# Chunked attention in front of a gated MLP: exponentials one head at a time on ScalarE, with the maximum as bias and the sum as by-product, heads paired by half, and all steps in a new order

## The chip, the core and the metric

One core of a Trainium2 chip runs the whole program. The metric is the device time of one execution in microseconds (us). Engines: PE is TensorE (PEld its weight loads), DVE is VectorE, ACT is ScalarE, POOL is GpSimd, SP is the engine that here only issues DMAs.

## The reference

A chunked attention with 8 heads, then a gated MLP that mixes along the sequence. Batch 4, 768 tokens, head size 64, chunks of 32 queries that see 8 memory keys and 56 keys around the chunk (16 to the left, 8 to the right).

```python
for c in range(nc):                                   # 24 chunks of 32 queries
    scores = scale * np.matmul(q_c, k_full.transpose(0, 1, 3, 2))
    scores = scores - np.max(scores, axis=-1, keepdims=True)
    a = np.exp(scores)
    a = a / (np.sum(a, axis=-1, keepdims=True) + 1e-09)
    out[:, :, c_start:c_end] = np.matmul(a, v_full)
...
h = gelu_tanh(x @ w_in)                               # x: (4, 768, 512), w_in: (512, 1024)
u, v = (h[..., :d_ff // 2], h[..., d_ff // 2:])
v_n = (v - mu) / np.sqrt(var + 1e-06) * g_ln
v_s = np.einsum('ts,bsd->btd', w_sg, v_n) + b_sg[None, :, None]
return (x + (u * v_s) @ w_out)
```

## The kernel before

The program is written as named steps, and the string `ORDER` says in which order they are recorded. Each engine then runs its own steps strictly in that order, so `ORDER` is a program for five queues at once. A star behind a name gives the step to the second engine it may run on.

**Attention** goes in 24 units `u` (4 batches, 6 tiles of 128 queries; unit `u` belongs to batch `u // 6`). A unit loads `q`, `k`, `v` (SP), and then runs
- `S`: 32 score matmuls into the PSUM tile `sav`, for 8 heads of 64 keys;
- `mx` the row maxima (DVE), `sb` the scores less the maximum, from `sav` to the SBUF tile `e` (DVE), `ex` one exponential over the 128x512 tile (ACT), `z` zeros for keys that do not exist at the ends of a sequence (POOL), `sm` the sums (DVE), `sa`/`sr` epsilon and reciprocal (DVE), `nm` the normalisation (DVE or POOL);
- `T` and `p`: four 128x128 transposes on PE and a copy (ACT or DVE) for the first ten units; `yt` and DMAs `E` for the others;
- `A`: 32 matmuls with `v`, again into `sav`;
- `xc` a copy to `x` (ACT), `xh` the high part (ACT), `xl` the low part (DVE or POOL). For four units (`DIRECT`) `xh` and `xl` read `sav` themselves.

There is one tile `sav` of two PSUM banks. Each bank holds the scores of four heads in its first half and the results of `A` in its second. Every step that touches `sav`, on PE, DVE or ACT, waits until the step of another engine that touched it last is through.

**The MLP** runs every product three times, on high and low parts (`HL`). Per batch: `V` six products of 12 matmuls with 512 columns, `U` eight of 12 with 384, `W` eight of 18, `O` eight of 12; behind each V and U come two ACT and two or more DVE steps (`v1` to `v9`, `u1` to `u4`), behind W `w1` to `w4`, behind O `o1` and the store. Names carry batch, half or tile, and block: `W001` is batch 0, half 0, block 1. Five PSUM tiles `mm` hold the products.

**Weights** arrive as float64 and are decoded by steps `d1` to `d9` on DVE, ACT and POOL: four blocks each of the two halves of `w_in` (`i1x`, `i0x`) and four of `w_out` (`ox`). The half `i1x` is needed by the first V. `ga`/`gb` split `w_sg`. `zz5` records five idle matmuls on `ident` that keep PE warm where there is nothing to do.

Of the kernel before, what the change touches and what calls it, by code (L numbers as in the profile page):

```python
# [39 lines left out]
d6i01 xh0 zz6 k5 d7i13 mx3 q5 xl0 sb3 nm2* A1 d8i13 ex3 S4 v4 xc1 d9i13* T2 xh1 k6 d2i03 V00 d1i03 q6 d4i03  # L40
xl1* p2 d2i02 d3i03 d6i03 d4i02 cbh sm3 mx4 V01 v100 sa3 sb4 sr3 v200 ex4 sm4 v300 v400 nm3* S5 v101 sa4
v500 A2 d7i01 v201 q7 T3 k7 mx5 v301 zz6 v5 sr4 xc2 d7i00 vx00 v401 p3 vy00 sb5 xh2 v600 v501 d8i00 S6 nm4*
ex5 xl2 d8i01 vx01 k8 mx6 A3 z5 q8 vy01 d9i01 sm5 T4 v6 xc3 V02 sa5 sr5 xh3 p4* d9i00 sb6 d6i02 v601 ex6
d5i03 z6 A4 v701 nm5* sm6 v801 S7 v7 xc4 sa6 sr6 xh4 mx7 q9 nm6* T5 k9 xl4 zz2 p5 sb7 xl3 V04 ex7 d1i02
d7i03 sm7 d3i02 sa7 sr7 d5i02 T6 d8i03 S8 v901* p6 v700 A5 v104 d7i02* k10 V03 v800 q10 nm7* v204 xh5 v8 mx8
v304 xl5 d9i03 xc5 d8i02 sb8 v404 ex8 v900 T7 v504 A6 sm8 d9i02 v102 S9 vx04 v9 xc6 p7* V05 v202 k11 ga50
q11 ga21 mx9 v302 vy04 sa8 sb9 v604 ga10 ga01 sr8 v402 nm8* ga31 U010 ga20 v502 ga41 v704 ex9 gb01 vx02 v804
vy02 sm9 U001 gb31* v602 g11 sa9 gb20* g00 v702 g30 sr9 v904* v802 U002 nm9 v105 gb10* ga11 v205 v902 g51
ga00 A7 v305 gb21* ga30 S10 gb11 v405 v103 g40 T8 v10 xc7 v203 gb00 k12 u1010 U003 v505 v303 q12 u2010 gb30
ga51 vx05 u1001 v403 u3010 gb51 vy05 u2001 u1002 U013 u4010 ga40 v605 v503 u3001 u1003 v705 u4001 v805 U000  # L50
vx03 u2003 vy03 v905* u3003 v603 mx10 v703 U012 u4003 v803 sb10 v903 u2002 ex10 p8* u3002 U011 sm10 u4002
sa10 d1o0 sr10 gb40* d3o0 T9 gb50* u1012 A8 d5o0 u1011 p9 W001 nm10* u2012 ro1 xc8 u2011 v11 u3012 u3011
gb41* d7o0 u4012 u1013 u4011 u2013 d8o0 W012 w1001 u3013 d2o1 u4013 d4o1 d1o1 w2001 d3o1 d6o1 w3001 d5o1
W002 w1012 w4001 ro2 w2012 d7o1 u1000 w3012 u2000 u3000 d9o0* d8o1 W000 u4000 w4012 w1002 d9o1 w2002 w3002
d1o2 d2o2 d3o2 w4002 W003 d4o2 w1000 d5o2 d6o2 w2000 ro3 d7o2* w3000 w4000* d8o2 W010 w1003 d9o2* w2003
w3003 d1o3 w4003* S11 d3o3 d2o3 w1010 W013 d4o3 q13 mx11 k13 w2010 d6o3 w3010 d5o3 sb11 w4010 A9 yt10 ex11
d7o3* S12 z11 v12 w1013 d8o3 W011 sm11 q14 d9o3* k14 sa11 w2013 sr11 mx12 w3013 nm11* sb12 O003 w1011 w4013
ex12 yt11 z12 w2011 Ec5 sm12 w3011 O000 o1003 w4011 sa12 sr12 nm12 out003 O011 Ed5 o1000 S13 o1011 Ea5 O013
mx13 sb13 ex13 S14 k15 o1013 Eb5 sm13 O012 mx14 sa13 sr13 nm13 O002 q16 o1012 k16 out012 out013 q15 O001
o1002 out000 yt12 out011 out002 yt13 sb14 O010 xh7 o1001 xh6 xl7* out001 ex14 xl6 xh8 sm14 V11 o1010 xl8*  # L60
out010 sa14 sr14 nm14* xc9 xh9 U102 v111 xl9* v211 v311 U101 u1102 v411 u2102 v511 u3102 u4102 V12 u1101
vx11 vy11 u2101 v611 u3101 v711 u4101 v811 v911* U100 v112 v212 v312 V13 v412 u1100 u2100 v512 u3100 u4100
vx12 vy12 v612 A10 v113 v712 V10 v213 v812 v13 xc10 v912 v313 xh10 v413 xl10 v513 A11 v110 vx13 vy13 S15
v210 v613 Ec6 xc11 V14 v713 v310 mx15 xh11 v410 v813 xl11* q17 v913* k17 v510 V15 v114 Ed6 sb15 vx10 v214
# [5 lines left out]
w1110 A13 w2110 k20 mx18 W111 w3110 q20 xc13 w4110* Ed7 Ea7 W102 w1111 w2111 w3111 w4111 v16 Ec7 O110 w1102  # L70
w2102 w3102 w4102 O112 o1110 Eb7 W100 o1112 out110 out112 yt16 W103 w1100 yt17 w2100 sb18 w3100 w4100* ex18
A14 w1103 z18 sm18 S19 v17 xc14 w2103 O111 sa18 k21 mx19 w3103 q21 sr18 w4103 sb19 ex19 nm18 O101 o1111 sm19
out111 sa19 sr19 nm19* O100 o1101 out101 O102 o1100 out100 A15 o1102 S20 out102 Eb8 O103 mx20 O113 q22 o1103
xh14 Ea8 xh12 xl14* xh13 xl12 V22 o1113 xl13* out113 v18 Ed8 V20 v122 v222 v322 Ec8 v422 U200 v522 v120 vx22
v220 out103 vy22 v320 v622 k22 U203 v420 u1200 u2200 v520 u3200 yt18 V21 u1203 u4200 xc15 sb20 xh15 yt19
ex20 xl15 u2203 vx20 sm20 u3203 A16 u4203 sa20 vy20 V23 v722 v620 v19 xc16 sr20 nm20* v822 xh16 v922* xl16*
v121 A17 v720 v221 V24 v820 Ea9 xc17 v920* v321 v123 v421 xh17 v223 xl17 v521 v323 U202 Ed9 vx21 v423 vy21
v523 v621 V25 v721 u1202 vx23 Ec9 v821 vy23 u2202 v623 u3202 v921 u4202 v723 v124 U211 Eb9 v823 v224 v923*
v324 v125 v424 U212 u1211 v225 v20 u2211 v325 v524 u3211 v425 U213 u1212 u4211 v525 yt20 A18 vx25 u2212
u1213 vx24 vy25 u3212 u2213 S21 v625 vy24 v21 xc18 u4212 v624 U201 u3213 mx21 q23 k23 u4213 v725 sb21 v825  # L80
A19 v724 u1201 ex21 v925 S22 u2201 v22 xc19 sm21 U210 v824 mx22 u3201 v924* u4201 sa21 W212 sb22 sr21 ex22
nm21 sm22 yt21 sa22 Ec10 sr22 nm22* W210 w1212 w2212 w3212 w4212 Ed10 u1210 W201 w1210 u2210 u3210 Ea10
u4210 w2210 w3210 W202 w1201 w4210* Eb10 w2201 w3201 w4201* W203 w1202 w2202 w3202 w4202* yt22 A20 w1203
W213 w2203 v23 xc20 w3203 w4203* A21 w1213 W200 w2213 w3213 w4213 W211 w1200 w2200 w3200 w4200 O201 w1211
# [531 lines left out]
```

## Time and profile before

| | |
|---|---|
| time, median of 3 runs | 407.88 us (403.1 to 409.68) |
| time of the profiled execution | 405.58 us |
| its span, first to last instruction | 403.8 us |
| mean granted TensorE clock | 0.992 |
| busy: PE, DVE, ACT, POOL | 379.8, 285.8, 160.8, 104.4 us |

The span is 1.8 us shorter than the time of that same execution. A row of the timeline reads: start, duration, engine, operation, tile written <- tiles read, and in brackets the idle time before it with what ended it. Durations of instructions that follow each other overlap by a little, so the distance from start to start is the better price of one. Each float32 matmul of the attention shows as two records (x64 for 32 matmuls).

### The profile page before, as it was taken

The numbers are of one execution on the slowest core, as the hardware profiler recorded it, in microseconds if no ns is written. First come the engines' busy times: TensorE is split into PE (matmuls) and PEld (weight loads), VectorE is DVE, ScalarE is ACT, GpSimd is POOL, SyncE is SP. The second block draws the span as 40 slices with busy tenths as digits, with TensorE's granted clock in tenths as the row PEclk, the third lists the DMA queues.
The fourth block names the chain that finished last, engine by engine and source line by source line (L and its number), as shares of the span: only waits on it lengthen the run. The fifth ranks groups of instructions, "written<-read, shape, count | busy, mean of one in ns | idle before, by whom it ended". The sixth has DMA issues, their size and how long they took to land.

```text
span 403.8 us, 11335 instructions
## 1 busy us (share of the span) xinstructions
PE 379.8 (94%) x4896; PEld 353.5 (88%) x4896; DVE 285.8 (71%) x558; ACT 160.8 (40%) x296; POOL 104.4 (26%) x113
## 2 busy tenths in 40 slices
PE   7788788999989999999999999998999999999996
PEld 6776677989979998789999988988999988999995
DVE  4996889999989567897637358895636456756532
ACT  4554646676532045653312046652211156532100
POOL 1433565463603021331121113321011224130000
PEclk9996999999999999999999999999999999999999
DMA  7998463542134360443143343242111320000022
GB/s 282 398 396 279 128 212 131 176 157 102 56 117 128 101 226 2 141 145 119 39 125 120 131 136 118 53 170 63 44 54 41 100 71 2 1 2 0 2 78 79
DMA packets 24530, 47.66 MB, mean 118 GB/s; under 512 B 4384, under 2 KB 13600, under 8 KB 24480
## 3 DMA queue, kind: packets, MB, share of 16 engines
q1 hardware_dynamic: 24480, 46.94, 35.0%
q8 instruction: 38, 0.62, 0.6%
q14 instruction: 12, 0.10, 0.1%
HBM read 36.96 MB, written 6.29 MB: 107 GB/s over the span
## 4 chain that ended last, share of the span: by engine, by line
PE 69%; DVE 19%; DMA 4%; issue 3%; ACT 3%; POOL 1%; SPq 0%; DVEq 0%; POOLq 0%; ACTq 0%
PE mmc L109 13%; PE mma L109 13%; PE mmd L109 12%; PE mmb L109 11%; PE mme L109 11%; PE sav L109 8%; DVE ga L109 2%; DMA y<-in_w_out 2%; DVE gb L109 2%; DMA rawc<-in_w_in 2%; DVE xo L109 1%; DVE rdb L109 1%; DVE w_sg_lo L109 1%; DVE eb L109 1%; ACT ga L109 1%
## 5 line engine op out<-in xcount | busy, mean ns | idle before, releaser
L109 PE MATMUL mma<-ident 128*128 128x128 f32 x136 | 18.3, 295 | 1.4 <-POOL mhalf L109 1.4
L109 PEld LDWEIGHTS mma<-ident 128*128 128x128 f32 x136 | 17.2, 208 | 1.7 <-POOL mhalf L109 1.4
L109 PEld LDWEIGHTS sav<-pt,va 64*64 64x64 f32 x512 | 8.5, 135 | 8.4 <-DVE ea L109 2.6
L109 PE MATMUL sav<-pt,va 64*64 64x32 f32 x512 | 9.4, 221 | 6.4 <-DVE eb L109 2.0
L109 PE MATMUL sav<-ka,qa 64*32 64x64 f32 x768 | 10.8, 231 | 4.3 <-DMA qa<-in_qs 1.5
L109 PEld LDWEIGHTS sav<-ka,qa 64*32 64x32 f32 x768 | 8.7, 109 | 6.2 <-issue 4.2
L109 PEld LDWEIGHTS sav<-pt,vb 64*64 64x64 f32 x512 | 9.1, 143 | 5.5 <-ACT w_in_hi L109 1.8
L109 ACT ACTIVATE eb<-eb 128x512 f32<-128x512 f32 x12 | 7.6, 630 | 16.0 <-DVE eb L109 15.9
L109 PE MATMUL sav<-pt,vb 64*64 64x32 f32 x512 | 10.1, 228 | 3.1 <-ACT w_in_hi L109 1.6
L109 ACT ACTIVATE gb<-gb 128x512 f32<-128x512 f32 (+1 forms) x14 | 8.8, 632 | 8.2 <-DVE gb L109 8.1
L109 PE MATMUL sav<-kb,qb 64*32 64x64 f32 x768 | 10.3, 224 | 1.9 <-DVE exb L109 1.9
L109 PEld LDWEIGHTS sav<-kb,qb 64*32 64x32 f32 x768 | 8.4, 105 | 3.4 <-DVE exb L109 2.0
L109 ACT ACTIVATE ga<-ga 128x512 f32<-128x512 f32 (+1 forms) x14 | 8.9, 633 | 6.0 <-DVE ga L109 5.9
L109 DVE SCALAR_TENSOR_TENSOR mmc<-mmc,g_half,b_half 128x384 f32<-128x384 f32 x8 | 5.0, 622 | 8.3 <-PE mmc L109 8.3
L109 POOL TENSOR_TENSOR rsc<-rsc,mhalf 128x1 f32<-128x1 f32 x8 | 4.4, 550 | 24.6 <-DVE rsc L109 24.6
L109 ACT COPY xa<-sav 128x512 f32<-128x512 f32 x9 | 5.2, 583 | 13.6 <-PE sav L109 10.9
L109 PE MATMUL mma<-w_in_hi,paira 128*128 128x512 f32 x32 | 9.9, 435 | 0.0
L109 PEld LDWEIGHTS sav<-pt,vc 64*64 64x64 f32 x512 | 8.3, 135 | 1.8 <-issue 1.2
L109 ACT ACTIVATE ea<-ea 128x512 f32<-128x512 f32 x12 | 7.6, 631 | 5.7 <-DVE ea L109 5.5
L109 POOL TENSOR_TENSOR rsb<-rsb,mhalf 128x1 f32<-128x1 f32 x8 | 4.4, 548 | 18.7 <-DVE rsb L109 15.9
L109 PE MATMUL sav<-pt,vc 64*64 64x32 f32 x512 | 9.2, 221 | 0.0
L109 POOL TENSOR_TENSOR rsa<-rsa,mhalf 128x1 f32<-128x1 f32 x8 | 5.0, 627 | 16.0 <-DVE rsa L109 16.0
(604 smaller groups left out, 1268.2 us busy)
## 6 DMA issues: line engine op xcount, KB each, us to landing
...
pt<-y SPq DMA_DIRECT2D x112, 32.0 KB, 1.9
...
```

Of the source, the lines that this page charges most:

```text
L109: return self.tc.keep_in_program_order(getattr(self.engine, name)(*args, **kw))
```

## The change

The exponential takes the scores from PSUM itself, one head at a time, eight instructions per unit on ACT: the negated maximum, times 0.125, is the bias of each, and each sums its row as a by-product. So `sb` and `sm` go; `mb` (a multiplication of 128x8 maxima) comes; missing keys get -1e30 in `sav`, on DVE ahead of the maximum, instead of zeros in `e` on POOL. Scores and results are paired by half of the heads instead of by neighbours, so that the copies out of `sav` keep its order. And `ORDER` is a new one throughout.

```diff
 ORDER = """
-ri10 k0 ri12 zz18 q0 ro0 v2 ri11 k1 g01 d1i10 d2i10 g31 d3i10 d4i10 d5i10 q1 d6i10 d1i12 ri00 d7i10* d3i12
-S0 d2i12 ri13 d8i10 zz19 d5i12 d4i12 d2o0 d9i10 mx0 k2 d4o0 sb0 d6o0 g21 ex0 d6i12 z0 d2i11 q2 d1i11 d4i11
+ri11 v0 q0 zz13 k0 k1 ri13 q1 v1 g40 d2i11 d1i11 d4i11 d3i11 d6i11 d5i11 d7i11* S0 d8i11 zz13 d9i11 k2 z0
+mx0 g31 q2 mb0 d2i13 ex0 d1i13 d4i13 S1 sa0 sr0 d3i13 d6i13 zz7 q3 mx1 nm0* ri12 mb1 ri03 ex1 d5i13 k3 T0
...
                         eng.matmul(
-                            s_v[CH * c:CH * c + CH, r, m], q[64 * r:64 * r + 64, m, c],
+                            s_v[CH * c:CH * c + CH, r, 2 * (m % 2) + m // 2], q[64 * r:64 * r + 64, m, c],
...
+        def no_keys(eng):
+            if tt == 0:
+                eng.memset(s_v[0:CH, :, :, 0:16], -1e30)
+            else:
+                eng.memset(s_v[P - CH:P, :, :, 56:64], -1e30)
+
         def largest(eng):
             eng.tensor_reduce(
-                mx.rearrange("p (r m) -> p r m", r=2), s_v, axis=AX.X, op=ALU.max
+                mx.rearrange("p (r m) -> p r m", r=2), s_v, axis=AX.X, op=ALU.max, negate=True
             )
-        def less(eng):
-            eng.tensor_tensor(
-                e_v, s_v, mx.rearrange("p (r m) -> p r m", r=2).unsqueeze(3).broadcast_to([P, 2, 4, KW]),
-                op=ALU.subtract,
-            )
...
+        def exps(eng):
+            for r in range(2):
+                for m in range(4):
+                    g = slice(4 * r + m, 4 * r + m + 1)
+                    eng.activation(
+                        e[:, 4 * r + m], s_v[:, r, m], AF.Exp, scale=0.125, bias=mx[:, g], accum_out=rd[:, g]
+                    )
...
+        if tt in (0, NTT - 1):
+            step(f"z{u}", no_keys, vector)
         step(f"mx{u}", largest, vector)
-        step(f"sb{u}", less, vector)
-        step(f"ex{u}", lambda eng: eng.activation(e, e, AF.Exp, scale=0.125), scalar)
-        if tt in (0, NTT - 1):
-            step(f"z{u}", no_keys, gpsimd)
-        step(f"sm{u}", lambda eng: eng.tensor_reduce(rd, e, axis=AX.X, op=ALU.add), vector)
+        step(f"mb{u}", lambda eng: eng.tensor_scalar_mul(mx, mx, 0.125), vector)
+        step(f"ex{u}", exps, scalar)
...
-        def by_pair(x):
-            return x[:, :, sl].rearrange("p (a h) t -> p a h t", h=2)
+        def by_half(x):
+            return x[:, :, sl].rearrange("p (h a) t -> p h a t", h=2)
...
-        step(f"xc{u}", lambda eng: eng.copy(by_pair(x32), av_x), scalar)
+        step(f"xc{u}", lambda eng: eng.copy(by_half(x32), av_v), scalar)
```

Three places of the new order follow, as rows of one engine's program. First DVE in the opening, before: the maximum `mxa` and the subtraction that writes `ea` of unit 0, and its sums `rda`, stand among the steps that decode blocks of `w_in` (`mc`, `exb`, ...) and `w_out` (`xo`).

```order
L109 TENSOR_REDUCE mxa<-sav 128x8
L109 TENSOR_TENSOR ea<-sav,mxa 128x512
L109 SCALAR_TENSOR_TENSOR xo<-y,xo 128x512
L109 SCALAR_TENSOR_TENSOR exc<-rawc,exc 128x512
L109 TENSOR_SCALAR exb<-rawb 128x512
L109 TENSOR_SCALAR mb<-rawb 128x512
L109 TENSOR_TENSOR mc<-mc,exc 128x512
L109 SCALAR_TENSOR_TENSOR exb<-rawb,exb 128x512
L109 SCALAR_TENSOR_TENSOR mb<-rawb,mb 128x512
L109 TENSOR_TENSOR w_in_lo<-mc,w_in_hi 128x512
L109 TENSOR_REDUCE rda<-ea 128x8
```

The same place of DVE's program in the changed kernel (here `mxa` scaled is the step `mb0`; the tiles `md`, `exd` belong to block i13):

```order
L108 MEMSET sav 32x2x4x16
L108 TENSOR_REDUCE mxa<-sav 128x8
L108 TENSOR_SCALAR mxa<-mxa 128x8
L108 TENSOR_SCALAR exd<-rawd 128x512
L108 TENSOR_SCALAR md<-rawd 128x512
L108 TENSOR_SCALAR rda<-rda 128x8
L108 RECIPROCAL rda<-rda 128x8
L108 SCALAR_TENSOR_TENSOR exd<-rawd,exd 128x512
```

Two rows of 128x512 per unit have gone, and the memset on `sav` has come.

Next ACT at the same place. Before, after the first decode steps, one exponential of unit 0 over all of `ea`:

```order
L109 ACTIVATE mc<-mc 128x512
L109 CAST w_in_hi<-ma 128x512
L109 ACTIVATE exc<-exc,e_bias 128x512
L109 ACTIVATE xo<-xo,e_bias 128x512
L109 ACTIVATE ea<-ea 128x512
L109 ACTIVATE exb<-exb,e_bias 128x512
```

In the changed kernel units 0 and 1 have eight each, with two decode steps between:

```order
L108 CAST w_in_hi<-mb 128x512
L108 ACTIVATE ea,rda<-sav,mxa 128x64 x8
L108 ACTIVATE exd<-exd,e_bias 128x512
L108 ACTIVATE md<-md 128x512
L108 ACTIVATE eb,rdb<-sav,mxb 128x64 x8
L108 COPY pt<-t 128x4x128
```

The decode of block i13 now stands behind the eight exponentials of unit 0.

Last, PE late in batch 1. Before, from `A14` and `S19` (rows 1 and 2) over four products O to `A15` and `S20`:

```order
L109 MATMUL sav<-pt,vc 64x32 x32
L109 MATMUL sav<-kb,qb 32x64 x32
L109 MATMUL mmb<-pairb,w_out_lo 128x384 x4
L109 MATMUL mmb<-pairb,w_out_hi 128x384 x8
L109 MATMUL mmd<-paira,w_out_lo 128x384 x4
L109 MATMUL mmd<-paira,w_out_hi 128x384 x8
L109 MATMUL mme<-paira,w_out_lo 128x384 x4
L109 MATMUL mme<-paira,w_out_hi 128x384 x8
L109 MATMUL mma<-paira,w_out_lo 128x384 x4
L109 MATMUL mma<-paira,w_out_hi 128x384 x8
L109 MATMUL sav<-pt,va 64x32 x32
L109 MATMUL sav<-ka,qa 32x64 x32
```

In the changed kernel `A14`, `S19`, one product O, `A15`, and the first of U:

```order
L108 MATMUL sav<-pt,vc 64x32 x32
L108 MATMUL sav<-kb,qb 32x64 x32
L108 MATMUL mme<-pairb,w_out_lo 128x384 x4
L108 MATMUL mme<-pairb,w_out_hi 128x384 x8
L108 MATMUL sav<-pt,va 64x32 x32
L108 MATMUL mmc<-paira,w_in_lo 128x384 x4
L108 MATMUL mmc<-paira,w_in_hi 128x384 x8
```

Between `S19` and the next step on `sav` PE had four products, and now has one.

More of the change, by code (lines that the diff above doesn't have):

```diff
@@ L40 @@
[L40 to L64, printed above, removed]
@@ L70 @@
[L70 to L84, printed above, removed]
@@ L95 @@
-w2310 w3310 w4310* O312 w1302 w2302 w3302 w4302* W301 o1312 out312 O310 w1301 w2301 w3301 w4301* O313 o1310
-out310 O300 o1313 out313 O303 o1300 out300 O311 o1303 out303 O302 o1311 out311 O301 o1302 out302 o1301
-out301
+ri11 v0 q0 zz13 k0 k1 ri13 q1 v1 g40 d2i11 d1i11 d4i11 d3i11 d6i11 d5i11 d7i11* S0 d8i11 zz13 d9i11 k2 z0
+mx0 g31 q2 mb0 d2i13 ex0 d1i13 d4i13 S1 sa0 sr0 d3i13 d6i13 zz7 q3 mx1 nm0* ri12 mb1 ri03 ex1 d5i13 k3 T0
+g21 zz3 d7i13* v2 p0 S2 sa1 ri10 sr1 d8i13 nm1 A0 d9i13 k4 mx2 T1 mb2 xh0 zz7 d1i12 ex2 xl0 d1i03 d2i03
@@ new lines @@
+d3i12 d2i12 S3 sa2 d4i03 sr2 d5i12 zz4 p1 nm2 k5 d4i12 q4 d6i03 T2 d3i03 d6i12 zz3 xc0 p2* A1 d7i12* d2i10
+zz9 d8i12 d1i10 v4 d4i10 d5i03 q5 d3i10 d9i12 mx3 g41 ri01 xc1 mb3 g51 ex3 A2 d6i10 d5i10 zz2 xc2 d7i03* S4
+xh2 d7i10* xh1 zz10 sa3 k6 mx4 d8i10 xl1 ri02 sr3 d8i03 xl2 v3 ri00 mb4 ex4 nm3 d9i10* T3 d1i01 V01 d2i01
+d3i01 d9i03 p3* d4i01 sa4 sr4 d6i01 d2i02 d1i02 V00 d4i02 d5i01 v101 d6i02 d3i02 nm4* v201 v301 d5i02 A3
+v100 d1i00 d2i00 d3i00 S5 d7i01 v200 xc3 v401 T4 v300 k7 z5 V02 d5i00 xh3 g00 d4i00 v501 xl3 d8i01 v400 p4
@@ new lines @@
+vx01 mx5 d9i01 vy01 v500 A4 mb5 v601 vx00 ex5 vy00 d7i02* v600 V03 v7 v701 q7 v700 xc4 v5 d6i00 v801 ro0
+v800 sa5 v901* cb xh4 v6 d7i00 sr5 d8i02 zz3 q6 xl4 v103 V04 d9i02* d8i00 v203 v900 v303 d9i00* v102 nm5*
+v403 ga21 U003 ga41 v202 ga40 v503 gb41 ga51 ga00 vx03 vy03 ga31 d2o0 v603 T5 v302 U000 gb31* d4o0 v703
+u1003 gb00 p5* v803 u2003 cbh v402 A5 u3003 u1000 u4003 u2000 S6 v8 xh5 v502 U002 xc5 xl5 u3000 z6 vx02
+u4000 gb40 mx6 vy02 V05 mb6 d6o0 v602 u1002 ex6 v903* v702 d1o0 v802 gb51 u2002 d3o0 sa6 S7 sr6 u3002 v902*
@@ new lines @@
+o1200 out200 Ea10 O202 w1211 Ec10 w2211 w3211 w4211* W210 o1202 q23 Ed10 O201 w1210 w2210 w3210 w4210* S22
+o1201 O210 mx22 mb22 ex22 A20 o1210 sa22 sr22 S23 nm22 v23 xc20 O212 yt22 z23 mx23 mb23 ex23 A21 o1212
+out212 O213 out202 sa23 sr23 nm23 yt23 Ea11 O203 o1213 O211 o1203 xh18 xh19 out203 xl18* xh20 out210 xl19*
+Ed11 xl20* V30 o1211 Eb11 V32 v130 v230 v330 out201 v430 Ec11 V31 v530 v132 vx30 v232 vy30 v332 v630 v22
+xc21 v432 out211 xh21 U300 v730 v532 v830 xl21* v930* V33 vx32 u1300 vy32 v131 v632 u2300 v231 u3300 v732
@@ L587, in _lay_out @@
             part = seq_v[:, :, at:at + KW].reshape(B, 2, 2, 2, KW, D)
-            vs[:, tt, :, :, c] = part.transpose(0, 2, 4, 3, 1, 5)
+            vs[:, tt, :, :, c] = part.transpose(0, 1, 4, 3, 2, 5)
     vs = vs.reshape(B, NTT, P, 4, 2, 2, D)
```

80 lines of the change are left out of this document (50 added, 30 removed).

## The prediction

> **What bounds the kernel now.** I read the page first, then busy time by stretches, then the chain that ended last.
>
> ```profile
> span 403.8 us, 11335 instructions
> ...
> PE 379.8 (94%) x4896; PEld 353.5 (88%) x4896; DVE 285.8 (71%) x558; ACT 160.8 (40%) x296; POOL 104.4 (26%) x113
> ...
> PE   7788788999989999999999999998999999999996
> ...
> DVE  4996889999989567897637358895636456756532
> ```
>
> PE is busy nearly throughout, and DVE is the next one; but DVE is at nine tenths only in the first third. Cut at the first V (36.1 us) and at the first W (96.4 us):
>
> ```profile
> 0.00:36.10 36.10, 27.31 (x596) 25.51 (x597) 26.66 (x50) 17.08 (x28) 12.46 (x18) 0.94 0.95 350
> 36.10:96.40 60.30, 53.93 (x1047) 47.04 (x1045) 55.75 (x107) 36.73 (x70) 31.87 (x31) 0.98 0.46 152
> ...
> 121.50:403.80 282.30, 275.45 (x3066) 258.53 (x3066) 180.60 (x360) 94.09 (x175) 51.14 (x58) 1.00 0.26 82
> ```
>
> Before the first V, PE's busy time is mostly idle matmuls. From 36.1 to 96.4 DVE is busy 55.8 of 60.3 us, so it leads there. From 121.5 us on PE is busy 275.5 of 282.3 us. These rows give what a step costs when nothing delays it (start to start, or merged pieces of the chain):
>
> ```profile
> 8.80 0.85 PE L109 MATMUL sav<-ka,qa 64*32 64x64 f32 x64 [1.55 <-DMA qa<-in_qs]
> 94.78 0.60 PE L109 MATMUL t<-ident,eb 128*128 128x128 f32 x4
> 95.31 1.14 PE L109 MATMUL sav<-pt,vc 64*64 64x32 f32 x64
> 96.37 0.44 PE L109 MATMUL mmc<-w_sg_hi,vha 128*128 128x384 f32 x1
> ...
> 141.26 2.08 PE mmc L109 x12
> 186.16 3.12 PE mmc L109 x18
> 198.63 1.85 PE sav L109 x117
> 234.15 2.79 PE mmd L109 x12
> ```
>
> T 0.53, A 1.07, S 0.79 (A and S together 1.85), U or O 2.08, V 2.79, W 3.12. For the whole program that is 24 x 2.79 + 64 x 2.08 + 32 x 3.12 + 24 x 1.86 + 10 x 0.53 = 350 us, so some 54 us of the span are not product work. The row at 96.37 is the first W, for which all engines must have done the opening's work; I measure the opening by it.
>
> **What goes and comes per unit.** DVE and ACT at unit 0, and the rows nearest to the new exponential:
>
> ```profile
> 11.33 0.68 DVE L109 TENSOR_REDUCE mxa<-sav 128x8 f32<-128x512 f32 x1
> 12.04 0.69 DVE L109 TENSOR_TENSOR ea<-sav,mxa 128x512 f32<-128x512 f32 x1
> 12.65 0.68 DVE L109 SCALAR_TENSOR_TENSOR xo<-y,xo 128x512 int32<-128x512 int32 x1
> 12.77 0.63 ACT L109 ACTIVATE ea<-ea 128x512 f32<-128x512 f32 x1 [0.60 <-DVE ea L109]
> 13.85 0.42 DVE L109 TENSOR_SCALAR exb<-rawb 128x512 int32<-128x512 int32 x1
> 14.19 0.42 DVE L109 TENSOR_SCALAR mb<-rawb 128x512 int32<-128x512 int32 x1
> 16.93 0.68 DVE L109 TENSOR_REDUCE rda<-ea 128x8 f32<-128x512 f32 x1
> ...
> 5.39 0.63 ACT L109 ACTIVATE ma<-ma 128x512 f32<-128x512 int32 x1 [3.38 <-DVE ma L109]
> 5.92 0.71 ACT L109 ACTIVATE exa<-exa,e_bias 128x512 int32<-128x512 int32 x1
> 84.21 0.50 ACT L109 ACTIVATE ua<-mmb 128x384 f32<-128x384 f32 x1
> 84.60 0.63 ACT L109 ACTIVATE ga<-ga 128x512 f32<-128x512 f32 x1
> 28.28 0.56 ACT L109 COPY xa<-sav 128x512 f32<-128x512 f32 x1
> ...
> L109 ACT ACTIVATE ga<-ga 128x512 f32<-128x512 f32 x12 | 7.6, 633 | 4.5 <-DVE ga L109 4.5
> L109 ACT ACTIVATE ub<-ub 128x384 f32<-128x384 f32 x6 | 3.2, 528 | 2.0 <-DVE ub L109 2.0
> ```
>
> - DVE loses `sb` and `sm`, 0.6 each from start to start (12.04 to 12.65), 1.2 us per unit and 28.8 us in all. `mb` and, in eight units, the memset come; no row shows the two, and I put them at 0.1 and 0.2, between nothing and one integer step of 0.34 (13.85 to 14.19): some 4 us.
> - ACT loses one activation (0.53) and gets eight. The price of one 128x64 from PSUM with a bias tile and a sum is not in the trace. From below: a 128x384 from PSUM starts 0.39 before the next (84.21 to 84.60); the two groups differ by 105 ns for 128 columns, 0.82 ns per column, so 64 columns take 0.13, and a bias tile adds 0.08 (0.63 against 0.71): 0.21, the sum free; eight are 1.7 us. From above: nothing overlaps, 633 ns less 448 columns is 0.27, plus 0.08: 0.35, eight are 2.8 us. I take 0.27, 2.15 us, because the exponential itself is near the lower row and the sum should cost something. ACT gains 1.6 us a unit, 39 us in all; it was at 161 of 404.
> - The copies out of `sav` move 512 elements per partition as before (0.56), only in another order: nothing, at most 0.1 either way on rows whose wait is `sav`.
> - SP's loads come in the new order. S0 waits for its loads (the row at 8.80), the first four then and now: `ri`, `k`, `ri`, `q` become `ri`, `v`, `q`, `k`, and `ri` and `v` are both 128 x 1024 words, so S0 stays at 8.8. The tail (last O, add, store) is the same.
>
> The Trainium skill, in "ScalarE: Activation LUTs", section "Rules for kernel authors", budgets about 0.3 us plus 0.83 ns per element for an activation with a bias pointer. By that rule, eight of 64 columns are 2.8 us, my upper end, and the sum below would end near 411 us. The trace's rows that follow each other come out lower, since one starts before the other has ended.
>
> **What it does to `sav`.** This is the part that speaks against the change. Reads of `sav` by one engine keep out the others:
>
> ```profile
> DVE mxb L109 <- ACT xa L109: 2.8, 1, 2.8
> ...
> 120.74 0.68 DVE L109 TENSOR_TENSOR eb<-sav,mxc 128x512 f32<-128x512 f32 x1
> 121.48 1.14 PE L109 MATMUL sav<-pt,va 64*64 64x32 f32 x64 [2.01 <-DVE eb L109]
> ...
> 181.77 1.32 PE L109 MATMUL sav<-pt,va 64*64 64x32 f32 x64 [0.70 <-DVE ea L109]
> ...
> 270.05 0.68 DVE L109 TENSOR_TENSOR eb<-sav,mxa 128x512 f32<-128x512 f32 x1
> 270.88 1.14 PE L109 MATMUL sav<-pt,vb 64*64 64x32 f32 x64 [0.73 <-ACT vhf L109]
> ```
>
> A maximum waits 2.8 us for a copy that reads the other half of the banks; three times PE waits with an A until the subtraction has read the scores (2.01, 0.70, 0.73 us; the last row names another ACT step, but the subtraction at 270.05 was the last on `sav`). Now the eight exponentials do that reading: from the end of S to the free tile it was 0.1 + 0.6 + 0.6 (`mx`, `sb`), and will be 0.1 + 0.6 + 0.15 + 2.15 + handovers, about 3.2 us, and 3.8 where an `xc` of 0.5 goes first.
>
> *The opening*, with these prices and 0.1 for a handover between engines. S0 8.8 to 9.6; memset, `mx0`, `mb0` to 10.75; `ex0` to 12.9; S1 to 13.8. ACT decodes two steps behind `ex0` (0.53, from 5.39 to 5.92, and 0.62 with its bias tile), DVE waits for them with one of its own, then `mx1` and `mb1` to 15.05; `ex1` to 17.2. S2 and A0 to 19.2, `mx2` to 19.95, `xh0` 0.5, `ex2` to 22.7; `xl0` may read `sav` only now, to 23.5. From there DVE has three integer steps, two small ones, six of 0.6, two integer steps and one of 0.6, 6.1 us, to 29.6, and `mx3` to 30.2. Then turn by turn on `sav`: `xc1` 30.8, `ex3` 33.0, A2 34.1, `xc2` 34.7, S4 35.6, `xh2` 36.2, `mx4` 36.95, `xl2` 37.6; the normalisation and the last low part of `w_in` give the first V at 39.0, three us later than now.
>
> But behind it PE has more to do at once: V, V, A3, S5, T4, V, A4, V to 53.7. The next V waits for `ex5` (53.15), `xc4`, two ACT steps, `xh4` and `xl4`, until 55.9; V, two U, T5, A5, S6 to 65.3, one U and the last V to 70.2. S7 waits for `xh5`, `xc5`, `xl5`, memset, `mx6`, `mb6`, one more ACT step and `ex6` (5.3 us and six handovers from 65.3), and ends at 72.0; three U, T6, S8 to 79.6, T7 and one U to 82.2; A6 waits for `ex8` (82.8) to 84.0; one U, T8, A7, S9, and the first W at 88.8. Before, one S, A and T more stood ahead of the first W (2.4 us), so 88.8 is held against 94.0: **5.2 us gained**. DVE's 1.2 us less per unit pay for it, and nine units lie in that stretch. About five exponentials stand on this path: at 1.7 us each the gain is 7.4, at 2.8 us 2.0.
>
> *Behind the first W* PE is full, and what counts is how much PE has between two steps on `sav`. In the new order: A8 behind S9, one W (0.9 us short of 4.2, with an ACT step ahead); A11 behind A10, one V (0.8); A15 behind S19 and A17 behind A16, one product of 2.1 each, with an `xc` in the way (1.5 each); A20 behind S22 (0.9); A21 behind S23 with memset and `xc` (1.8). Sum 7.4 us of new waits. The three old ones, 3.4 us, go, as their places now have 6 us or more. Net **4 us lost**; with six exponentials of 1.7 us on it 1.3, of 2.8 us 7.9. What is late next is PE itself, so these waits are not given back.
>
> **Sum**, against the profiled execution: 405.6 - 5.2 + 4.0 = 404.4, say **404 us**; bounds by the exponential 399.5 (405.6 - 7.4 + 1.3) and 411.5 (405.6 - 2.0 + 7.9). The median of the runs shown, 407.88, is 2.3 above that execution; a difference of 2% is about what a measurement here tells from none, so the forecast is no change.
>
> **Rivals.**
> - *DVE alone sets the opening, and the exponential is cheap.* For: 92% of DVE between first V and first W. Then ten units at 1.1 us net, over 0.92, give 12 us in place of 5, and at 1.7 us per unit the later waits cost 1.3: 394.9. Against: the tile `sav` must be read out in turn. It would show as DVE again over 90% ahead of the first W, and a first W near 82.
> - *Slower: reading out each sum occupies ACT.* If a head takes 0.45 us from start to start, `ex` is 3.6, 1.45 more at five places in the opening and six behind: 404.4 + 16 = 420. It decides from 3.0 us per unit on, 0.375 per head, just above my upper row: there the sum passes 413.7, 2% over 405.6. For it: no row shows what a sum costs. Against: it would have to cost more than the exponential.
> - *The new order does not fill PE.* Between A1 (28.1) and S4 (34.8) PE has one A and eleven idle matmuls, and it may lose its clock as before, where the first four matmuls of V took 2.06 us and later four 1.09:
>
> ```profile
> 36.10 2.06 PE L109 MATMUL mma<-w_in_hi,paira 128*128 128x512 f32 x4
> 40.24 1.09 PE L109 MATMUL mmb<-w_in_hi,paira 128*128 128x512 f32 x4
> ```
>
> That costs 1 to 3 us and stays within the range.
>
> **Chances.** The forecast with its bounds and the third rival, within 2%: 0.61. DVE alone: 0.25; its time is 2.6% faster. ACT's read-out: 0.14. For 8 in 10 the range reaches from below the first rival's time, which is not sharp to 3 us, to some way into the second: 392 to 414. Faster 0.25, same 0.61, slower 0.14.
>
> **What would show it.** Right: groups of 128x64 activations at 0.25 to 0.3 us; PE waits of 1 to 2 us ahead of matmuls that write `sav`, ended by ACT, where now DVE ends them; the first W near 89 us; DVE about 25 us less, ACT about 40 more. Wrong: a first W after 94 (the chain through `sav` is longer than worked out) or before 84; less than 3 us of waits on `sav` after it; ACT over 220 us.

## The result, and the profile after

The changed kernel takes **431.29 us** (median of 4 runs, 430.39 to 432.21) against 405.49 us for the kernel before beside it: **ratio 1.066, 95% interval 1.056 to 1.076**, slower. The forecast was 404 us, with a range from 392 to 414. The profiled execution took 430.39 us with a span of 428.6 us, 24.8 us above that of before.

From the page after, then the busy time by stretches, cut at the first V (44.06 us) and at the first W (102.9 us):

```profile
span 428.6 us, 11647 instructions
PE 390.9 (91%) x4892; PEld 362.4 (85%) x4892; DVE 269.3 (63%) x548; ACT 201.5 (47%) x653; POOL 100.1 (23%) x102
...
PE   6777979959899999799999899799999699999996
...
DVE  3675998996793555567754447876444548675442
...
PEclk8996999988999999699999989989999999999999
```

```profile
0.00:44.00 44.00, 32.52 (x669) 30.14 (x670) 24.98 (x51) 25.01 (x95) 8.33 (x14) 0.88 0.71 248
44.00:102.90 58.90, 50.63 (x838) 43.72 (x836) 52.56 (x104) 42.27 (x136) 30.74 (x28) 0.94 0.50 167
...
102.90:428.60 325.70, 307.73 (x3391) 288.59 (x3388) 191.76 (x394) 134.21 (x424) 60.99 (x61) 0.98 0.26 83
```

VectorE is busy 16.5 us less (some 25 were forecast) and ScalarE 40.7 us more (about 40). On VectorE the 24 scalings `mb` and the eight memsets take 9.0 us (some 4 were forecast), and 14 normalisations run there instead of 7, since the new order gives fewer of them to GpSimd (10.8 us in place of 4.9). But PE has holes, and its granted clock, 0.992 on the mean before, is 0.964. The first W:

```profile
102.88 0.43 PE L108 MATMUL mme<-w_sg_hi,vha 128*128 128x384 f32 x1
```

Held against 94.0 before (96.37 less 2.4, as in the prediction), the opening is **8.9 us longer** instead of 5.2 shorter. Behind it are 325.7 us against 309.8, **15.9 us more** instead of 4. Together 24.8.

What PE waited for behind the first W (tile waited for, by which step its wait ended; us in total, times, longest), in the kernel before:

```profile
PE sav L109 <- DVE eb L109: 2.0, 1, 2.0
PE sav L109 <- issue: 1.5, 1, 1.5
PE sav L109 <- ACT vhf L109: 0.7, 1, 0.7
PE sav L109 <- DVE ea L109: 0.7, 1, 0.7
```

and after:

```profile
PE sav L108 <- ACT eb L108: 7.7, 4, 2.9
PE sav L108 <- ACT ea L108: 5.6, 3, 2.6
PE sav L108 <- ACT xa L108: 1.0, 1, 1.0
```

14.3 us of waits, all on `sav`, 13.3 of them ended by the exponentials, in place of 4.9: 9.4 us more. The other 6.5 of the 15.9 agree with the granted clock: 0.98 over 325.7 us is 6.5 us of lost full-speed time (two digits, so give or take 1.6), where the kernel before shows 1.00. One of these places, A11, on ACT, DVE and PE (the eight heads run from 173.68 to 176.00, the first is shown):

```profile
171.03 0.57 ACT L108 COPY xa<-sav 128x512 f32<-128x512 f32 x1
171.63 0.69 DVE L108 TENSOR_REDUCE mxb<-sav 128x8 f32<-128x512 f32 x1 [0.46 <-ACT xa L108]
172.77 0.87 DVE L108 TENSOR_SCALAR mxb<-mxb 128x8 f32<-128x8 f32 x1
173.68 0.31 ACT L108 ACTIVATE eb<-sav,mxb 128x64 f32<-128x64 f32 x1 [1.42 <-DVE mxb L108]
173.89 0.19 ACT L108 ACTIVATION_READ_ACCUMULATOR eb<-sav,mxb 128x1 f32 x1
...
176.00 0.63 ACT L108 ACTIVATE ga<-mmd 128x512 f32<-128x512 f32 x1
```

```profile
176.20 1.93 PE L108 MATMUL sav<-pt,vc 64*64 64x32 f32 x64 [2.87 <-ACT eb L108]
178.06 2.07 PE L108 MATMUL mmb<-w_in_hi,pairb 128*128 128x512 f32 x4
...
182.93 1.10 PE L108 MATMUL mmc<-w_in_hi,paira 128*128 128x512 f32 x4
```

The reader sees the whole loss in one place. A head costs 0.29 us from start to start, 0.20 for the exponential and 0.09 for a record of its own that reads the sum out; eight are 2.32. Ahead of them stand a copy, the maximum, two other VectorE steps and the scaling, which took 0.87 and not 0.1. The wait is 2.87 us, and then A11 takes 1.93 in place of 1.14, and four matmuls 2.07 in place of 1.10: PE comes out of the wait at half clock (granted clock 0.50 from 176.20 to 181.00).

### The profile page after: what moved, and what is told of

It is laid out like the page before. It is cut to its first block, busy times and chain, and to the rows that moved or that the text cites. A ratio compares the mean times of both kernels' runs of the same rounds, so it can differ in the third digit from the quotient of the medians.

```text
span 428.6 us, 11647 instructions
## 1 busy us (share of the span) xinstructions
PE 390.9 (91%) x4892; PEld 362.4 (85%) x4892; DVE 269.3 (63%) x548; ACT 201.5 (47%) x653; POOL 100.1 (23%) x102
## 4 chain that ended last, share of the span: by engine, by line
PE 65%; ACT 14%; DVE 12%; DMA 4%; SPq 3%; issue 1%; POOL 0%; DVEq 0%; ACTq 0%
PE mmc L108 12%; PE mma L108 11%; PE mmb L108 11%; PE mme L108 11%; PE mmd L108 10%; PE sav L108 9%; ACT eb L108 5%; ACT ea L108 3%; SPq L108 3%; DVE mxb L108 1%; DMA kb<-in_ks 1%; DMA rawb<-in_w_in 1%; DMA out<-xa 1%; DVE ga L108 1%; DVE gb L108 1%
## 5 line engine op out<-in xcount | busy, mean ns | idle before, releaser
L108 PE MATMUL mma<-ident 128*128 128x128 f32 x142 | 22.8, 322 | 3.4 <-issue 2.0
L108 PEld LDWEIGHTS mma<-ident 128*128 128x128 f32 x142 | 20.9, 232 | 4.2 <-issue 2.6
L108 PEld LDWEIGHTS sav<-pt,vc 64*64 64x64 f32 x512 | 10.8, 163 | 15.7 <-ACT eb L108 8.7
L108 PE MATMUL sav<-pt,vc 64*64 64x32 f32 x512 | 11.8, 245 | 13.3 <-ACT eb L108 7.7
L108 ACT ACTIVATE ea<-sav,mxa 128x64 f32<-128x64 f32 x32 | 9.5, 323 | 14.6 <-DVE y L108 9.0
L108 ACT ACTIVATE eb<-sav,mxc 128x64 f32<-128x64 f32 x32 | 9.5, 326 | 8.5 <-PE t L108 5.6
L108 ACT ACTIVATE eb<-sav,mxb 128x64 f32<-128x64 f32 x32 | 9.5, 324 | 3.7 <-DVE mxb L108 3.7
L108 ACT ACTIVATE eb<-sav,mxa 128x64 f32<-128x64 f32 x32 | 9.5, 327 | 3.3 <-DVE mxa L108 3.2
L108 ACT ACTIVATE ea<-sav,mxb 128x64 f32<-128x64 f32 x32 | 9.5, 323 | 3.3 <-DVE mxb L108 3.3
L108 DVE TENSOR_REDUCE mxb<-sav 128x8 f32<-128x512 f32 x8 | 5.5, 688 | 7.8 <-ACT paira L108 4.7
```

The lines of the kernel that those rows point to most:

```text
L108: return self.tc.keep_in_program_order(getattr(self.engine, name)(*args, **kw))
```

## The experiments

Numbered in the order in which they ran. Times are medians; "first W" is the time of the first W's first matmul in the one profiled execution, "behind" that execution's span less this time. For kernels in the order of before, 2.4 us are to be taken off the first W and added behind. The changed kernel and 14 run the same program up to the first W, and it stands at 102.9 and 100.3: in this column a difference of less than some 3 us says nothing.

| | time, us | ratio to before, 95% interval | first W | behind |
|---|---|---|---|---|
| kernel before | 405.49 | 1 | 96.4 (less 2.4: 94.0) | 307.4 (309.8) |
| changed kernel | 431.29 | 1.066 (1.056 to 1.076) | 102.9 | 325.7 |
| 1 new order, old softmax | 412.73 | 1.019 (1.013 to 1.026) | 96.9 | 314.3 |
| 2 old order, eight exponentials | 431.91 | 1.065 (1.058 to 1.073) | 108.1 | 322.6 |
| 3 changed, sums on VectorE | 419.85 | 1.035 (1.030 to 1.040) | 97.3 | 319.6 |
| 4 changed, one exponential | 410.91 | 1.011 (1.005 to 1.017) | 95.8 | 314.0 |
| 5, 9 changed, idle matmuls in the waits | 430.22, 425.49 | 1.059, 1.049 (1.044 to 1.055) | 102.2, 100.3 | 325.8, 323.1 |
| 6, 10, 14 changed, order mended behind | 428.97, 432.95, 426.49 | 1.057, 1.066, 1.050 (1.043 to 1.057) | 101.8, 102.1, 100.3 | 328.9, 329.5, 321.6 |
| 13 changed, less decoding | 428.36 | 1.055 (1.049 to 1.062) | 98.0 | 329.3 |
| 8, 11, 12 new order mended, one exponential | 417.83, 413.94, 413.04 | 1.028, 1.019, 1.017 | 93.0, 95.5, 95.3 | 323.4, 316.6, 315.7 |
| 7, 15, 16 old order, one exponential | 407.33, 410.20, 410.88 | 1.003 (1.000 to 1.007), 1.011, 1.013 | 100.4, 100.2, 101.8 | 305.2, 308.3, 305.9 |
| 17 old order, one exponential from unit 10 on | 403.66 | 0.997 (0.993 to 1.001) | 95.8 | 305.6 |

Theories: the eight exponentials hold `sav` too long (1), or the new order is at fault (2).

### 1 and 2: order and exponentials apart

```diff
 # 1: new order kept
-step(f"mb{u}", lambda eng: eng.tensor_scalar_mul(mx, mx, 0.125), vector)
+step(f"mb{u}", less, vector)        # e = sav - mx, as before; T9 and yt16 a few places earlier
-eng.activation(e[:, 4*r+m], s_v[:, r, m], AF.Exp, scale=0.125, bias=mx[:, g], accum_out=rd[:, g])
+eng.activation(e, e, AF.Exp, scale=0.125)   # and the sums on VectorE
 # 2: changed kernel's steps, ORDER of before: sb -> mb, sm out, z ahead of mx
```

> The changed kernel with the softmax of before: one step on VectorE subtracts the maximum out of sav into e, one exponential of 128x512 works inside e, VectorE sums. Numbering by half, memset in sav and the new order stay; two steps move ahead by a few places so that e is not overwritten too early (T9, yt16). Theory 1, the eight exponentials hold sav: the hold after a score step falls from 3.6 us (4.4 with a copy ahead) to about 1.6 (2.2), so of the 14.3 us of PE waits on sav behind the first W under 3 us remain, the granted clock behind it returns to 0.99 or more, the first W comes near 95 us, and the time is 400 to 408 us. Theory 2, the new order itself is at fault: 423 to 432 us, with PE waits at the same places, ended by VectorE.

> The changed kernel's code (eight exponentials, sums as by-product, numbering by half, memset in sav) run in the order of the kernel before; the scaling of the maxima stands where the subtraction stood, the memset ahead of the maximum. Theory 1, the exponentials hold sav: the old order leaves PE about 1.5 us of other work between two steps on sav at its tight places, so there are as many waits as in the changed kernel or more, and it is 415 to 435 us. Theory 2, the new order is at fault: 402 to 410 us, like the kernel before.

In 2, unit 5's exponentials, at their old place behind S6, read unit 6's scores. Waits of PE behind the first W in 2:

```profile
PE sav L106 <- ACT eb L106: 6.9, 3, 3.0
PE sav L106 <- ACT ea L106: 6.6, 3, 3.0
```

Both theories hold a part. The exponentials are the larger: in the old order they cost as much as the whole change, with 13.5 us of waits on `sav`. (2 also has the memset on `sav` and the pairing by half, but so has 7 below, in the same order, which is 0.3% above the kernel before.) But 1 missed its 400 to 408: the new order costs some 2% with the old softmax too, 4.5 us of it behind the first W; the first W is 2.9 us later than 94.0, no more than that column scatters. What in the order costs this was not tried.

### 3 and 4: the length of the hold

```diff
 # 3
-    ... AF.Exp, scale=0.125, bias=mx[:, g], accum_out=rd[:, g]
+    ... AF.Exp, scale=0.125, bias=mx[:, g]       # tensor_reduce(rd, e) ahead of sa
 # 4: one maximum per query, one exponential
-mx.rearrange("p (r m) -> p r m", r=2), s_v, axis=AX.X, op=ALU.max, negate=True
+mx[:, 0:1], s_v, axis=AX.XYZ, op=ALU.max, negate=True
+eng.activation(e.rearrange("p (r m) k -> p r m k", r=2), s_v, AF.Exp, scale=0.125, bias=mx[:, 0:1])   # sums as in 3
```

> The changed kernel without the sum as by-product: the eight exponentials have no accumulator, and VectorE sums each row of e (128x512 to 128x8, 0.69 us) ahead of the step sa. Theory 1, with the read-out of each sum a part of the hold (0.09 of 0.29 us per head, 0.7 us of 2.3 per unit): a head takes 0.20 us, PE waits on sav fall by about 0.7 us at each of some seven places behind the first W and some six ahead of it, and each us of wait carries up to one more in lost clock: 418 to 426 us. Rival, the read-out costs nothing on the path, or VectorE's sums cost as much again: 428 to 434 us.

> The changed kernel with one exponential of 128x512 out of sav per unit. Its bias is one maximum per query over all eight heads in place of one per head (the softmax is the same in exact arithmetic), and VectorE sums each row of e. The order stays. Theory 1, the length of the hold decides: the exponential holds sav 0.6 us in place of 2.3, the hold is about 1.9 us (2.5 with a copy), PE waits on sav behind the first W fall from 14.3 to under 4 us, the clock returns to about 0.99, and the time is 397 to 408 us. Theory 2, the new order: 423 to 432 us.

The same unit 13 in both, on ACT (in 3 the eight heads are one row), and what PE waits for behind the first W in 3, then in 4:

```profile
167.24 1.75 ACT L108 ACTIVATE eb<-sav,mxb 128x64 f32<-128x64 f32 x8 [1.43 <-DVE mxb L108]
```

```profile
166.41 0.69 ACT L108 ACTIVATE eb<-sav,mxb 128x512 f32<-128x512 f32 x1 [0.70 <-DVE mxb L108]
166.99 0.59 ACT L108 ACTIVATE ga<-mmd 128x512 f32<-128x512 f32 x1
```

```profile
PE sav L108 <- ACT eb L108: 6.3, 4, 2.1
PE sav L108 <- ACT ea L108: 3.1, 3, 1.5
```

```profile
PE sav L108 <- ACT eb L108: 2.1, 3, 0.9
...
PE sav L108 <- ACT ea L108: 1.1, 1, 1.1
```

Eight heads without sums take 1.75 us from the first start to the last end, one exponential 0.69. From start to start that is 1.6 and 0.58, and, in the changed kernel, 2.32 us per unit; in rising order the spans are 409.8, 416.9 and 428.6: the first microsecond more costs 7 us and the next 0.7 another 11.7, although VectorE has to sum in 3 and 4. So, taken away in this sequence, **reading the sums out is the dearest part of the change**. 4 ended 3 us above its 408, near 1: with a short hold, 1 to 2% are left, as with the old softmax in the new order. In the profiled execution of 4, 4.2 us of it are a stand of PE within S9 whose cause was not tried (last section).

### 5 and 9: the clock

```diff
+def warm_t(n):                     # idle 128x128 matmuls into the transposes' bank (ahead of A2 into an mm bank)
+    for _ in range(n): tensor.matmul(t_ps[:, 0:P], ident, ident, start=True, stop=True)
-V13 xc10 ... A11                   # ORDER; 9: zt11, and likewise at S13, A14, A17, A20, A21, A2
+V13 xc10 ... zt11 A11
```

> The changed kernel with idle 128x128 matmuls recorded ahead of eight steps that wait for sav (S13 6, A11 18, A14 10, A15 3, A17 16, A20 7, A21 13, into the transposes' bank that is free by then; A2 14, into a free mm bank), some 0.13 us each, a little less than the waits. Nothing else moves, so the steps on sav can start no earlier. Theory 1, idle PE of 1.5 us and more lowers the granted clock for the next microseconds: the half-speed rows behind A2, A11, A14 and A17 go (A11 from 1.93 to 1.14), the granted clock behind the first W goes from 0.98 to 1.00 and the time to 420 to 427 us. Rival, the clock drops for another reason (or idle matmuls delay the steps as much): 429 to 434 us.

> The experiment with idle matmuls again, with fewer of them: there an idle matmul took 0.23 us and not 0.13, and ahead of A11 they ran 1.1 us past the moment at which sav was free. Now S13 2, A11 11, A14 6, A17 9, A20 4, A21 7 and A2 9. Theory 1, each wait of 1.5 us and more halves the clock of the next 3 to 5 us: A11 to U112 takes 9.6 us in place of 12.3, the part behind the first W gains 3 to 6 us, the opening about 1: 424 to 428 us. Rival, the half clock costs nothing of its own: 429 to 432 us.

5 settled nothing: the granted clock behind the first W was 1.00, but at A11 the idle matmuls ran 1.1 us past the moment at which `sav` was free, and that part of the span was as long as in the changed kernel (325.8 us). In 9 they ended just before `sav` was free:

```profile
172.07 2.62 PE L107 MATMUL t<-ident 128*128 128x128 f32 x22
175.11 1.14 PE L107 MATMUL sav<-pt,vc 64*64 64x32 f32 x64 [0.42 <-ACT eb L107]
176.17 1.20 PE L107 MATMUL mmb<-w_in_hi,pairb 128*128 128x512 f32 x4
...
186.87 0.86 PE L107 MATMUL sav<-ka,qa 64*32 64x64 f32 x64
```

From A11 to S14 it is 11.8 us in place of 14.5 (176.20 to 190.72). Behind the first W 2.6 us went (3 to 6 were expected), and 1.3% of the time in all (425.49 us in place of 431.29), though no step on `sav` could start earlier. The granted clock there is 0.99, 3.2 us of lost full-speed time in place of 6.5, which fits. So the wait at A11 cost itself, 2.87 us, and nearly as much again, 2.7 us, in half clock; the 14.3 us of waits together cost at least 2.6 us more in this way. Not all of the 1.3% is this: the first W moved by 2.6 us, and it stood at 100.3 in experiment 14 too, which changes nothing ahead of it.

### 6, 10 and 14: could the order hide the waits?

`X Y` means that step X now stands ahead of Y, and its later steps where they then belong.

```diff
 # 6:  W011 A8 S10 | V14 A11 | yt16 z18 | U202 A15 | U200 U201 A17 | O203 A20 | O213 A21
 # 10: as 6 without U202 and with: S19 O103 | U301 V33 | U303 A23 | k8, k14, out003, out001, Ec7 earlier
 # 14: only V14 A11 (k14 earlier) | O203 A20 | O213 A21 | U301 V33 | U303 A23
```

> The changed kernel with the order mended only behind the first W: W011 ahead of A8, V14 ahead of A11, U202 ahead of A15, U201 between A16 and A17, O203 ahead of A20, O213 ahead of A21, and the transposition yt16 ahead of the maximum of unit 18 (the exponentials of unit 18 write the tile e that yt16 reads, and waited 9.03 us for it). The eight exponentials stay. Theory 1, PE has too little between two steps on sav: of 14.3 us of waits behind the first W some 3 remain (S13, and the rest at A17), the clock behind it returns to 0.99 or more, another 5 us: 413 to 420 us, the first W unchanged near 103. Rival, the work that is drawn forward is missed later, or something else bounds this part: 425 to 432 us.

> The changed kernel, eight exponentials, with the order mended behind the first W and with what the first try lacked. As there: W011 ahead of A8 (now with the load v11 behind A8, which it had to follow, and the maximum of unit 10 behind four steps that it held up), V14 ahead of A11, U201 ahead of A17, O203 ahead of A20, O213 ahead of A21. New: A15 keeps its place and O103 goes between S19 and O111; U301 ahead of V33 and U303 ahead of A23 fill where A21's parts come late; the loads k8 and k14, the stores out003 and out001 and the exchange Ec7 are issued earlier on SP. Theory 1, the waits behind the first W are a matter of how much PE has between two steps on sav: of 14.3 us some 2 remain and the clock there returns to 0.99: 411 to 417 us. Rival, work moved forward is missed later: 420 us or more.

> The changed kernel, eight exponentials, with only those moves of the two earlier tries that left no new wait behind: V14 ahead of A11 (with the load k14 earlier), O203 ahead of A20, O213 ahead of A21, U301 ahead of V33, U303 ahead of A23. Theory 1: the waits at A11, A20 and A21 (2.87, 1.27 and 2.07 us) go, with the half clock behind A11 (2.7 us); up to 2 us come back at S14 to A12, where PE now arrives ahead of the exchange of units 12 and 13: 422 to 426 us. Rival, all that is moved forward is missed later: 428 us or more.

In 6 the load `v11` stood ahead of A8, which so multiplied with unit 11's `v`; in 10 O103 stood behind the first step that puts batch 2's values into the tile it reads, and so read some of them. Both times are those of such kernels. Waits that 6 shows:

```profile
245.75 2.03 PE L106 MATMUL sav<-pt,vc 64*64 64x32 f32 x64 [3.45 <-ACT ea L106]
```

```profile
241.29 0.71 DVE L106 STREAM_TRANSPOSE y<-ea 128x512 f32<-128x512 f32 x1 [6.10 <-DMA pt<-y]
```

```profile
274.88 1.19 PE L106 MATMUL sav<-pt,vb 64*64 64x32 f32 x64 [3.58 <-DMA vb<-in_vs]
```

A14 (first row) waits for unit 18's exponentials, these for the transposition of unit 16 that reads the same tile `e` (second row), and this one for the exchange DMAs of units 14 and 15: a chain that no PE work between S18 and A14 shortens. A16 (third row) comes earlier and finds its load not there. So the rival holds for 6 and 10: work moved forward was missed later. 14, which keeps the harmless moves, loses the waits at A11, A20 and A21, gets 0.9 back at S15 and A16 each, and is 4.1 us shorter behind the first W, just outside its 422 to 426.

### 13: what sets the opening?

```diff
-step("d5" + tag, d5, vector)
-step("d6" + tag, d6, vector)
+step("d5" + tag, lambda eng: None, vector)
+step("d6" + tag, lambda eng: None, vector)
```

> The changed kernel with two of the decode steps on VectorE left out, d5 (low bits) and d6 (sign), 0.68 us each, in all twelve blocks of weights (so the weights are positive and less exact); ten of the blocks come ahead of the first W, 13.6 us of VectorE's work. Theory A, in the opening VectorE's own work sets the time: the first W comes 8 us or more earlier, before 95 us, and the time is under 423 us. Theory B, the turns on sav set it, and VectorE mostly waits for exponentials (12 of its 23 us of idle time there end with them): the first W moves by less than 5 us, to 98 to 102, and the time is 425 to 431 us.

13 leaves out two decode steps (low bits, sign) in all twelve blocks of weights. What VectorE waited for up to the first W, in the changed kernel and in 13 (ahead of these rows stands the first load, 5 us in both):

```profile
...
DVE mxb L108 <- ACT paira L108: 4.7, 1, 4.7
DVE paira L108 <- ACT ea L108: 2.5, 1, 2.5
DVE rdb L108 <- ACT eb L108: 2.0, 2, 1.3
DVE rda L108 <- ACT ea L108: 1.9, 1, 1.9
```

```profile
...
DVE pt L108 <- PE t L108: 3.6, 2, 2.6
DVE mxb L108 <- ACT paira L108: 3.2, 1, 3.2
DVE paira L108 <- ACT ea L108: 2.5, 1, 2.5
DVE rdb L108 <- ACT eb L108: 2.3, 2, 2.0
```

VectorE's work up to the first W falls by 11.7 us (65.8 busy in place of 77.5), and the first W comes 2 to 5 us forward (98.0 against 102.9, or 100.3 in experiments 9 and 14); 3.6 us are lost again behind it. A hold 0.7 us shorter, in 3, brings 3 to 6, with more work on VectorE. Theory B, then, at the edge of its range: in the changed kernel the turns on `sav` set the opening and VectorE waits for them, for exponentials (6.9 us) and for a high part out of `sav` (4.7). With a short hold it may be the other way round; that was not tried, but in 1 VectorE is busy 93% from the first V on, against 89% in the changed kernel:

```profile
38.20:96.90 58.70, 52.07 (x838) 44.90 (x836) 54.72 (x107) 34.35 (x65) 30.65 (x27) 0.91 0.47 155
```

### 7, 8, 11, 12, 15, 16, 17: a version that is faster?

All have one exponential per unit and one maximum per query (units 10 to 23 only in 17).

```diff
 # 7:  ORDER of before, ex5 ahead of S6          # 15: 7 with mb, ex right behind mx
 # 8:  ORDER of 6   # 11: k8, k14, out003, out001, Ec7 earlier; V14 A11; S19 O103; U200 U201
 # 12: 11, d3i11 ahead of d4i11 (16: 15), and both:
-step(f"mb{u}", lambda eng: eng.tensor_scalar_mul(...), vector)
+step(f"mb{u}", lambda eng: eng.mul(mx[:, 0:1], mx[:, 0:1], 0.125), scalar)
 # 17: kernel before; if u >= 10: largest over XYZ, less -> scaling, ex from s_v with bias
```

> The order of the kernel before, with one exponential of 128x512 out of sav per unit (one maximum per query over all eight heads as bias, sums on VectorE); unit 5's exponential stands ahead of S6, since it now reads sav. VectorE does 0.6 us less per unit than before. Theory 1, what made the change slow is the hold of 2.3 us by eight exponentials and, for some 6 us, the new order, and the direct read as such is good: the hold is 1.9 us where it was 1.5, and VectorE's 0.6 us over nine units bring the first W forward by 1 to 5 us: 399 to 406 us, no slower than before. Rival, the exponential's place in ScalarE's queue, behind other steps, holds sav as long as in the second experiment: 408 to 416 us.

> The new order as mended behind the first W in the experiment of this call that keeps eight exponentials, with one exponential of 128x512 out of sav per unit (one maximum per query over all heads as bias, sums on VectorE). Theory 1: the fourth experiment's 411 us less its waits behind the first W (0.36, 0.89, 1.05, 0.87 us) less a little clock: 405 to 409 us. Rival, the waits that go come back elsewhere: 410 to 413 us.

> The new order with one exponential of 128x512 out of sav per unit (one maximum per query over all eight heads as bias, sums on VectorE), and seven moves: loads k8 and k14, stores out003 and out001 and exchange Ec7 earlier on SP, V14 ahead of A11, O103 between S19 and O111, U201 ahead of A17. Theory 1: the opening ends as in the run that kept it (first W near 91 to 93 us), and behind it the fourth experiment's 307 us from S10 on lose its 3 to 4 us of waits: 398 to 403 us, 1 to 2% faster than before. Rival, the opening falls back to the first W of 96 us of the fourth experiment, or the moves cost elsewhere: 404 to 409 us.

> The kernel of this call with one exponential, and two more moves: the scaling of the maximum by 0.125 goes from VectorE to ScalarE, right ahead of the exponential, and the first two decode steps on ScalarE change places, so that the load of the activation table does not wait for VectorE (5.67 us in the changed kernel, 0.73 in the one before). Theory 1, the scaling costs the hold a turn in VectorE's queue (0.14 to 1.09 us a time in the changed kernel): some 0.3 us less hold in nine units of the opening and 1 us at the start, 2 to 4 us faster than its neighbour. Rival, ScalarE's handling of it costs as much: within 1 us of its neighbour.

> The order of the kernel before with one exponential of 128x512 out of sav per unit, as in the seventh experiment, but with the scaling and the exponential right behind the maximum (behind the transposition that last reads the same tile e, where that comes later). Theory 1, in the seventh experiment the exponential came late in ScalarE's queue and held sav in the opening (first W at 100.4 us, 4 us late; behind it 2.2 us were gained): the first W returns to 95 to 98 us and the time is 400 to 404 us, 0.5 to 1.5% faster than before. Rival, ScalarE's other steps are late by as much: 405 to 409 us.

> The same with the scaling of the maximum on ScalarE instead of VectorE, right ahead of the exponential. Theory 1, it spares the hold a turn in VectorE's queue: 0.5 to 2 us faster than its neighbour. Rival, ScalarE's own price (0.2 us and its place in the queue) takes that back: within 0.5 us or slower.

> The kernel before, its order untouched, with one exponential of 128x512 straight out of sav in units 10 to 23 only (one maximum per query over all eight heads as bias; the sums stay on VectorE); units 0 to 9 keep the softmax of before. Theory 1, from the seventh experiment: with a short hold the direct read gains behind the first W (2.2 us there, since VectorE's subtraction of 0.6 us is gone and three waits of PE end earlier) and loses only in the opening, which is now as before: the first W at 96 to 97 us and 401 to 404 us, 0.3 to 1% faster than before. Rival, what was gained behind the first W there came only from being late before it: 404 to 407 us.

8 has 6's misplaced load, 11 and 12 have 10's misplaced O103, and all three end above 4, so a mended new order with a short hold was not measured; 8 and 11 lie above both of their ranges, 15 just above its rival's. Scaling on ScalarE moved the time by less than 1 us either way (12 against 11, 16 against 15). In the old order (7) the direct read with a short hold is no measurable change, though the time is above the 399 to 406 expected: it gains 2.2 us behind the first W and loses 4 ahead of it. 15 shows that this loss does not come from the exponential's place in ScalarE's queue; from where it comes stays open. 17 keeps the opening as it was. PE waits behind the first W in 17:

```profile
PE sav L109 <- ACT eb L109: 1.7, 2, 0.9
PE sav L109 <- ACT ea L109: 1.1, 2, 0.8
```

2.8 us in place of 4.9, and 305.6 us behind in place of 307.4. At a ratio of 0.997 (0.993 to 1.001) it is the best of all, but not measurably better than the kernel before. So behind the first W reading `sav` directly costs nothing as such; its length does.

## Why the prediction was wrong

- **The price of the exponential was right**: 0.27 us per head was taken, 0.29 measured, well inside 0.21 to 0.35. But "the sum should cost something" hid that the sum is a separate 0.09, and that leaving it out would give 11.7 of the 24.8 us back (experiment 3). The Trainium skill's rule ("ScalarE: Activation LUTs", "Rules for kernel authors"), which the prediction weighed, gives 2.8 us for eight; the traces have 2.32 with the sums and 1.6 without.
- **The opening, minus 5.2 us, failed by 14, and it failed as a walk.** This is the step of the prediction that failed first: the path through `sav` was added up with every step at its shortest price, ready when its turn came. Forecast against measured: S1 13.0 and 14.38, S2 17.3 and 19.94, A2 33.1 and 36.27, first V 39.0 and 44.06, first W 88.8 and 102.88. Two steps that were priced at 0.1 and 0.6, and a wait of PE that half clock follows:

```profile
10.68 1.09 DVE L108 TENSOR_SCALAR mxa<-mxa 128x8 f32<-128x8 f32 x1
...
14.97 1.54 DVE L108 SCALAR_TENSOR_TENSOR exd<-rawd,exd 128x512 int32<-128x512 int32 x1 [0.20 <-ACT exd L108]
```

```profile
36.27 1.93 PE L108 MATMUL sav<-pt,vc 64*64 64x32 f32 x64 [2.74 <-ACT eb L108]
```

  That the level was wrong and not only the exponential is seen in 4, 8, 11 and 12: with 0.6 us per unit the walk's own slope (5.4 us for 1.1 us per unit) would have given a first W near 81; they reached 93 to 96 (2.5 to 4.2 us of it, in 4, 11 and 12, the stand of PE within S9). "DVE's 1.2 us less per unit pay for it" failed too: VectorE's steps stand behind `sa` and the maximum in its queue, so it could not use the time that it saved.
- **Behind the first W, plus 4 us, was right in kind and four times too small.** The waits came where they were forecast, five of six longer (A8 2.10 for 0.9, A11 2.87 for 0.8, A17 2.55 for 1.5, A20 1.27 for 0.9, A21 2.07 for 1.8; only A15 shorter, 0.62 for 1.5), and two were not seen (A14 1.75, S13 1.03): 14.3 in place of 7.4. Where nothing stood between (A20, A21) the forecast hold was short by 0.3 us only; where VectorE and ScalarE had other steps between maximum and exponential it was short by 1 to 2. A14's wait came through the tile `e`, which the prediction did not follow: the step that reads the scores out, before the subtraction and now the exponentials, must wait until that tile is free, and only then does the 2.3 us of reading begin (unit 18's exponentials start at 243.19, PE has `sav` at 245.72).
- **The clock was dismissed** as 1 to 3 us in one place of the opening. It is 12 us of full-speed time over the span (0.992 to 0.964), 6.5 of it behind the first W, and experiment 9, where idle matmuls in the waits bring the mean from 0.964 to 0.988, shows that it comes from the waits.
- **The rivals.** "Slower" was there, 420 us, with the right place and the wrong trigger: it asked for a head of 0.375 us or more, and the head took 0.29. What decided was the hold around the eight heads, and the half clock that some of the waits leave behind. "DVE alone sets the opening" fell (first W 102.9, not 82). "The new order does not fill PE" was put at 1 to 3 us; experiment 1 measured the order at about 2%, some 6 to 7 us, and experiment 4 at about 1%; the cause stays open.
- **A reading.** VectorE's row before is at nine tenths not only in the first third, but in two later slices too; no term of the sum rests on it.
